# A fused attention, Fourier-mixing and gated-MLP kernel: DFT constants loaded in six pieces, the first weights' conversions and a value maximum at other steps, and the gated MLP's product on VectorE with its first tap and its cast on ScalarE

## The chip, the core and the metric

The kernel runs on one core of a Trainium2 chip. The metric is the device time of one launch in microseconds (us); lower is better. The core has a matrix engine (TensorE; PE in the profile, with PEld for its weight loads), VectorE (DVE), ScalarE (ACT), GpSimd (POOL) and a queue that only issues DMAs (SyncE, SP). Each engine takes its instructions in program order, and waits on semaphores for the others. SBUF is the on-chip memory, PSUM the memory that matmuls write.

## The reference, cut to what matters

Attention over 2 batches and 8 heads with 768 positions of width 64, where a query sees only the keys that have its own nearest centroid; then a mixing layer (two Fourier transforms, real part) with a normalised MLP; then a gated MLP.

```python
def _attn_ref(q, k, v, centroids):
    q_assign = np.argmax(np.einsum('bhsd,hcd->bhsc', q_n, c_n), axis=-1)
    k_assign = np.argmax(np.einsum('bhsd,hcd->bhsc', k_n, c_n), axis=-1)
    mask = q_assign[:, :, :, None] == k_assign[:, :, None, :]
    scores = np.where(mask, scale * np.matmul(q, k.transpose(0, 1, 3, 2)), -1000000000.0)
    attn = np.exp(scores - np.max(scores, axis=-1, keepdims=True))
    attn = attn / (np.sum(attn, axis=-1, keepdims=True) + 1e-09)
    return np.matmul(attn, v)

def _moe_ref(x, w_ch1, w_ch2):
    mixed = np.real(np.fft.fft(np.fft.fft(x, axis=1), axis=2))
    u = x + mixed
    un = (u - mu) / np.sqrt(var + 1e-06)
    return u + np.maximum(un @ w_ch1, 0.0) @ w_ch2

def _moe2_ref(x, w_in, conv_w, w_out):          # kernel = 3 taps over the sequence
    h = np.maximum(x @ w_in, 0.0)
    for k in range(K):
        conv_out += conv_w[k][None, None, :] * hp[:, k:k + S, :]
    gate = 1.0 / (1.0 + np.exp(-conv_out))
    return h * gate @ w_out
```

## The kernel before, in words

Every float32 product is made of three passes (`pass3`): each operand is split into a high part (rounded to the matrix engine's reduced float32) and a low part (what is left), and high x high, high x low and low x high are summed in PSUM.

**The attention loop** is written out by hand. It runs over steps n = -8 to 105. Of the 96 tiles (16 heads, 6 blocks of 128 queries) step n makes the scores of tile n + 8 (`score_max`: four matmuls, L530 and L532, into a PSUM slot `s`, and the row maximum by VectorE, L535, into `m`), the exponentials of tile n (`score_exp`: four matmuls, L564 and L566, into a slot `t`, read by ScalarE, L572), the split of the probabilities of tile n - 1 (ScalarE's cast L584, and the subtraction L592 by GpSimd or, for the tiles in `LO_ON_DVE`, by VectorE), and the product with V of tile n - 3 (18 small matmuls, L604). The slots for `s`, `t` and side work are three, used in turn, so a matmul into a slot waits until the slot's last reader is done. That reader is VectorE's maximum for an `s`.

Side work is hung on steps with `at(list, step, function)`; in a step the lists come in the order `pre`, `mid` (within `score_max`), `aft`, `post`, `fill`. The heads are prepared in pairs m, one pair every 12 steps (k = 12 m - 24): `load_raw` (q and k, 768 KB) at k, `prep_sims` (12 matmuls against the centroids, L404, then L408 and L410 on VectorE) at k + 5, `prep_hi` and `prep_lo` (the split of q and k; L461 and L463 on VectorE) at k + 8 to k + 11, `load_v` (384 KB into `vraw`) at k + 14, `v_max` (the largest value of V in each partition, L489 on VectorE) at k + 16, `v_turn` (a matmul that spreads it, L495) and `v_step` 0 to 3 (L502 to L508) at k + 18, `v_step` 4 and 5 (L510 on ScalarE, L512 on VectorE) at k + 22 and k + 25.

**The first weights** arrive as 64-bit numbers. Four half pieces q = 0 to 3 of two weight tiles are turned into float32 inside the loop: `ahead_start` loads a piece, five operations of `from64` (L283, L284 on VectorE, L285 on ScalarE, L286, L288 on VectorE) stand at the five steps of `AHEAD_STEPS`, and `ahead_store` writes the piece to DRAM one step later. The pieces stand in the tile `ahead`, which takes the place of `early`, the first pairs' raw and split q and k.

**The mixing** of batch 0 is hung on steps 54 to 76 (`plan`). Its constants `DC` (two planes, high and low, of 3342 columns) are loaded by GpSimd's DMA queue in the loop, and `OD` after them.

**The MLPs** follow with an automatic order. In the gated MLP, `mlp2_up(b, f)` makes one of 16 blocks of 128 hidden units: two halves of 12 matmuls each into PSUM (`u`), a relu by ScalarE into `h` (L820), three taps along the sequence into `cv` (L822 to L824), a sigmoid (L825), the product with `h` (L826), and the split into `gH` (L828) and `gL` (L829), which `down` reads in 18 matmuls (`acc`). The weights of a block are split by ScalarE (L792) and GpSimd (L794, `wlb`). `mlp2_up` runs two blocks ahead of `down`. During the first blocks `gate_in(1)` turns batch 1 (`xT`, `x`, L858 to L868), and `down` of a batch's last block copies its six results out (`y`).

## Time and profile before

| | us |
|---|---|
| median of 3 runs | 743.91 (739.0 to 745.26) |
| the profiled execution | 743.33 |
| its span, first to last instruction | 741.5 |
| PE busy in the span | 694.9 (94%) |
| DVE busy | 531.4 (72%) |
| ACT busy | 346.8 (47%) |
| POOL busy | 269.6 (36%) |
| mean granted TensorE clock | 0.984 of full speed |

The profiled execution's time is its span and 1.8 us around it. Busy time is a union of modelled intervals: matmuls overlap, so a stretch with PE busy throughout is not PE at its peak. The attention loop ends at about 296 us, batch 0 of the first MLP with the mixing of batch 1 beside it at about 395, the gated MLP starts at about 589.

### The profile page before, as it was taken

The numbers are of one execution on the slowest core, as the hardware profiler recorded it, in microseconds if no ns is written. First come the engines' busy times: TensorE is split into PE (matmuls) and PEld (weight loads), VectorE is DVE, ScalarE is ACT, GpSimd is POOL, SyncE is SP. The second block draws the span as 40 slices with busy tenths as digits, with TensorE's granted clock in tenths as the row PEclk, the third lists the DMA queues.
The fourth block names the chain that finished last, engine by engine and source line by source line (L and its number), as shares of the span: only waits on it lengthen the run. The fifth ranks groups of instructions, "written<-read, shape, count | busy, mean of one in ns | idle before, by whom it ended". The sixth has DMA issues, their size and how long they took to land.

```text
span 741.5 us, 12519 instructions
## 1 busy us (share of the span) xinstructions
PE 694.9 (94%) x5090; PEld 618.4 (83%) x5090; DVE 531.4 (72%) x753; ACT 346.8 (47%) x493; POOL 269.6 (36%) x189
## 2 busy tenths in 40 slices
PE   8898999898898998989999999999999999999996
PEld 5697788787797886878988999999999888898984
DVE  7778989799977997999389938764111268777664
ACT  3476868586457687424234423443222233333321
POOL 8064544446244454121132012222332254444441
PEclk9999999999799999999999999999999999999999
DMA  7738678463532332324013421430000000002002
GB/s 213 183 71 213 183 198 248 121 179 79 151 78 58 89 107 95 114 77 179 29 44 127 156 72 61 166 114 1 1 0 1 1 0 1 1 1 85 1 1 85
DMA packets 19937, 66.47 MB, mean 90 GB/s; under 512 B 2868, under 2 KB 5928, under 8 KB 16808
## 3 DMA queue, kind: packets, MB, share of 16 engines
q1 hardware_dynamic: 19448, 61.93, 28.9%
q0 software_dynamic: 432, 3.75, 1.5%
q8 instruction: 40, 0.66, 0.4%
q14 instruction: 17, 0.14, 0.1%
HBM read 40.94 MB, written 5.77 MB: 63 GB/s over the span
## 4 chain that ended last, share of the span: by engine, by line
PE 45%; DVE 35%; DMA 5%; POOL 5%; ACT 4%; issue 3%; SPq 1%; POOLq 0%; DVEq 0%
DVE m L535 5%; PE acc L82 5%; DVE gH L828 5%; PE acc L80 5%; PE acc L81 5%; PE up L82 5%; PE up L80 5%; PE up L81 5%; DMA vraw<-v 4%; POOL cv L826 3%; PE av L604 3%; DVE cv L823 2%; DVE cv L824 2%; PE t L564 2%; PE s L530 2%
## 5 line engine op out<-in xcount | busy, mean ns | idle before, releaser
L592 POOL TENSOR_TENSOR p<-p,p 128x768 f16<-128x768 f32 x61 | 108.3, 1778 | 113.2 <-ACT p L584 83.0
L572 ACT ACTIVATE p<-t,cbias 128x768 f32<-128x768 f32 x92 | 82.7, 899 | 51.7 <-PE t L566 50.9
L535 DVE TENSOR_REDUCE m<-s 128x1 f32<-128x768 f32 x96 | 90.1, 943 | 11.7 <-PE s L532 6.6
L80 PE MATMUL up<-un,wha 128*128 128x384 f32 x248 | 84.2, 340 | 1.5 <-DVE firste L809 0.7
L82 PE MATMUL up<-un,wla 128*128 128x384 f32 x248 | 83.9, 339 | 1.6 <-DVE wla L794 1.6
L794 POOL TENSOR_TENSOR wla<-wa,wha 128x1024 fp32r<-128x1024 f32 x16 | 38.5, 2407 | 126.5 <-ACT wha L792 126.5
L81 PE MATMUL up<-un,wha 128*128 128x384 f32 x248 | 83.8, 338 | 0.0
L809 DVE SCALAR_TENSOR_TENSOR hL<-up,hH 128x384 fp32r<-128x384 f32 x62 | 34.2, 551 | 65.5 <-ACT hH L808 65.4
L604 PEld LDWEIGHTS <-p 128*128 128x128 f16 x1728 | 60.1, 99 | 18.0 <-issue 15.5
L584 ACT CAST p<-p 128x768 f16<-128x768 f32 x88 | 73.0, 830 | 1.4
L604 PE MATMUL av<-V,p 128*128 128x65 f16 x1728 | 71.7, 196 | 2.0 <-POOL p L592 2.0
L80 PE MATMUL acc<-wha,hH 128*128 128x512 f32 x186 | 73.6, 396 | 0.0
L82 PE MATMUL acc<-wha,hL 128*128 128x512 f32 x186 | 72.6, 391 | 0.0
L81 PE MATMUL acc<-wla,hH 128*128 128x512 f32 x186 | 72.5, 390 | 0.0
L564 PE MATMUL t<-X 128*128 128x384 f32 x192 | 55.6, 371 | 15.5 <-DVE m L535 14.1
L808 ACT ACTIVATE hH<-up 128x384 fp32r<-128x384 f32 x62 | 30.5, 491 | 75.7 <-PE up L82 75.6
L530 PE MATMUL s<-X 128*128 128x384 f32 x192 | 56.8, 377 | 5.9 <-DVE m L535 4.9
L828 DVE CAST gH<-cv 128x768 fp32r<-128x768 f32 x16 | 35.4, 2212 | 31.3 <-POOL cv L826 31.3
L792 ACT CAST wha<-wa 128x1024 fp32r<-128x1024 f32 x31 | 32.6, 1050 | 52.2 <-PE acc L82 46.2
L826 POOL TENSOR_TENSOR cv<-cv,h 128x768 f32<-128x768 f32 x16 | 25.5, 1591 | 78.0 <-ACT cv L825 78.0
L564 PEld LDWEIGHTS t<-X 128*128 128x128 f32 x192 | 31.8, 193 | 24.2 <-DVE m L535 15.2
L566 PE MATMUL t<-Y 98*128 98x384 f32 x192 | 50.9, 347 | 0.1
(314 smaller groups left out, 1644.3 us busy)
## 6 DMA issues: line engine op xcount, KB each, us to landing
rawa<-w SPq DMA_DIRECT2D x14, 1024.0 KB
rawb<-w SPq DMA_DIRECT2D x8, 1024.0 KB
raw<-qk SPq DMA_DIRECT2D x7, 768.0 KB
X<-G SPq DMA_DIRECT2D x14, 384.0 KB
Y<-G SPq DMA_DIRECT2D x14, 384.0 KB
DC<-dft POOLq DMA_DIRECT2D x2, 1671.0 KB, 7.0
vraw<-v SPq DMA_DIRECT2D x8, 384.0 KB
out<-y SPq DMA_DIRECT2D x12, 256.0 KB
```

Of the source, the lines that this page charges most:

```text
L80: T.matmul(o, sH, mH, start=start, stop=False)
L81: T.matmul(o, sH, mL, start=False, stop=False)
L82: T.matmul(o, sL, mH, start=False, stop=stop)
L530: T.matmul(t[:, c, 0:384], X[:, 0, sl], X[:, 1, 384 * c:384 * c + 384], start=True, stop=False)
L535: V.tensor_reduce(m6s[h][:, i:i + 1], t[:, :, 0:384], AX.XY, ALU.max, negate=True)
L564: T.matmul(t[:, c, 0:384], X[:, 1, sl], X[:, 0, 384 * c:384 * c + 384], start=True, stop=False)
L566: T.matmul(t[:, c, 0:384], Y[0:98, 1, sl], Y[0:98, 0, 384 * c:384 * c + 384], start=False, stop=True)
L572: A.activation(p, t[:, :, 0:384], AF.Exp, bias=cbias, scale=0.125)
L584: A.copy(p16[:, 0], p32s[n])
L592: eng.tensor_sub(p16[:, 1], p, p16[:, 0])
L604: T.matmul(o, p16[:, k, 128 * j:128 * j + 128], v16[:, i, h % 2, 65 * part:65 * part + 65], start=(i + j + k + part == 0), stop=(i == 5), ...
L828: V.tensor_copy(g[0], t)
```

## The change

Four edits. The DFT constants: each plane is loaded in three pieces, at steps 8, 20, 21 and 32, 33, 44 in place of two whole planes at 20 and 32, and `OD` at 45 in place of 33. The conversions: piece 0 at steps 10, 10, 11, 11, 13; pieces 1 to 3 twelve steps earlier than before, at 17, 29 and 41 where pieces 0 to 2 stood; the loads and stores follow them. `v_max` at k + 17, `v_turn` and `v_step` 0 to 3 at k + 19, one step later each. The gated MLP: the first tap goes from VectorE's `tensor_scalar` to ScalarE's copy with a scale, the product with `h` from GpSimd to VectorE, and the cast to `gH` from VectorE to ScalarE.

```diff
-DFT_LOADS = (20, 32)
+DFT_LOADS = (8, 20, 21, 32, 33, 44)
...
-AHEAD_STEPS = [12 * q + n for q in range(4) for n in (17, 17, 18, 18, 22)]
+AHEAD_STEPS = [10, 10, 11, 11, 13] + [12 * q + n for q in range(1, 4) for n in (5, 5, 6, 6, 10)]
...
-            at(fill, k + 16, v_max, m)
-            at(mid, k + 18, v_turn, m)
+            at(fill, k + 17, v_max, m)
+            at(mid, k + 19, v_turn, m)
             for i in range(4):
-                at(aft, k + 18, v_step, m, i)
+                at(aft, k + 19, v_step, m, i)
...
             if n in DFT_LOADS:
-                i = DFT_LOADS.index(n)
-                G.dma_start(out=DC[:, i], in_=dft[:, i])
-            if n == DFT_LOADS[1] + 1:
+                i, part = divmod(DFT_LOADS.index(n), 3)
+                part = slice(*((C_CS, C_SS), (C_SS, C_CD), (C_CD, C_END))[part])
+                G.dma_start(out=DC[:, i, part], in_=dft[:, i, part])
+            if n == DFT_LOADS[-1] + 1:
                 G.dma_start(out=OD, in_=odd)
...
         t = gp.tile([128, S], F32, tag="cv", bufs=2, name=f"cv{b}{f}")
-        V.tensor_scalar(t, h2[:, 0:S], cw[:, 3 * f:3 * f + 1], None, ALU.mult)
+        A.activation(t, h2[:, 0:S], AF.Copy, scale=cw[:, 3 * f:3 * f + 1])
         V.scalar_tensor_tensor(t, h2[:, 1:S + 1], cw[:, 3 * f + 1:3 * f + 2], t, ALU.mult, ALU.add)
         V.scalar_tensor_tensor(t, h2[:, 2:S + 2], cw[:, 3 * f + 2:3 * f + 3], t, ALU.mult, ALU.add)
         A.activation(t, t, AF.Sigmoid)
-        G.tensor_mul(t, t, h2[:, 1:S + 1])
+        V.tensor_mul(t, t, h2[:, 1:S + 1])
         g = hs[1, b, f] = [gp.tile([128, S], F32R, tag=n, bufs=2, name=f"{n}{b}{f}") for n in ("gH", "gL")]
-        V.tensor_copy(g[0], t)
+        A.copy(g[0], t)
         V.tensor_sub(g[1], t, f32(g[0]))
```

Three places show what the order of instructions becomes.

VectorE at steps 52 to 54 (m is a row maximum, vsc the maximum of V, ahead the piece under conversion, mx and eq the centroid step). Before:

```order
L535 TENSOR_REDUCE m_10_2425<-s_2426 128x1
L489 TENSOR_REDUCE vsc_2466<-vraw_2385 128x1
L617 SCALAR_TENSOR_TENSOR U<-av_2163,vsc_1468,d_2387 128x6x64
L535 TENSOR_REDUCE m_10_2425<-s_2469 128x1
L283 TENSOR_SCALAR ahead<-ahead 128x512
L284 SCALAR_TENSOR_TENSOR ahead<-ahead 128x512
L408 TENSOR_REDUCE mx_2518<-sim_2505 128x24
L410 TENSOR_TENSOR eq_2520<-sim_2505,mx_2518 128x384
L535 TENSOR_REDUCE m_10_2425<-s_2527 128x1
L502 TENSOR_REDUCE vsc_2466<-s_2527 128x1
```

After the change:

```order
L535 TENSOR_REDUCE m_10_2435<-s_2436 128x1
L617 SCALAR_TENSOR_TENSOR U<-av_2173,vsc_1531,d_2397 128x6x64
L535 TENSOR_REDUCE m_10_2435<-s_2477 128x1
L408 TENSOR_REDUCE mx_2524<-sim_2511 128x24
L410 TENSOR_TENSOR eq_2526<-sim_2511,mx_2524 128x384
L489 TENSOR_REDUCE vsc_2528<-vraw_2395 128x1
L535 TENSOR_REDUCE m_10_2435<-s_2535 128x1
L535 TENSOR_REDUCE m_10_2435<-s_2574 128x1
L502 TENSOR_REDUCE vsc_2528<-s_2574 128x1
```

The maximum of V has moved behind one more row maximum and the two centroid operations, and the conversion is gone from here; in the three rounds before this one the conversion stays, and its L286 comes behind the row maximum that follows L489.

VectorE at steps 10 to 13 after the change (before, the same rows stood without the four of ahead):

```order
L535 TENSOR_REDUCE m_3_691<-s_692 128x1
L283 TENSOR_SCALAR ahead<-ahead 128x512
L284 SCALAR_TENSOR_TENSOR ahead<-ahead 128x512
L617 SCALAR_TENSOR_TENSOR U<-av_413,vsc_175,d_651 128x6x64
L535 TENSOR_REDUCE m_3_691<-s_737 128x1
L286 SCALAR_TENSOR_TENSOR ahead<-ahead 128x512
L461 TENSOR_TENSOR G_649<-raw_337,G_649 128x768
L535 TENSOR_REDUCE m_3_691<-s_790 128x1
L592 TENSOR_TENSOR p_11_796<-p_759,p_11_796 128x768
L535 TENSOR_REDUCE m_3_691<-s_824 128x1
L288 SCALAR_TENSOR_TENSOR ahead<-ahead 128x512
L512 SCALAR_TENSOR_TENSOR V_1_157<-vraw_395,vsc_525,V_1_157 128x12x64
```

Four operations are added between the row maxima of these steps.

VectorE in the last two blocks of the gated MLP, from the end of block 14 to that of block 15. Before:

```order
L828 CAST gH_7664<-cv_7658 128x768
L829 TENSOR_TENSOR gL_7665<-cv_7658,gH_7664 128x768
L822 TENSOR_SCALAR cv_7721<-h_7690,cw 128x768
L823 SCALAR_TENSOR_TENSOR cv_7721<-h_7690,cw,cv_7721 128x768
L824 SCALAR_TENSOR_TENSOR cv_7721<-h_7690,cw,cv_7721 128x768
L828 CAST gH_7727<-cv_7721 128x768
L829 TENSOR_TENSOR gL_7728<-cv_7721,gH_7727 128x768
```

After the change, on VectorE:

```order
L827 TENSOR_TENSOR cv_7662<-cv_7662,h_7631 128x768
L830 TENSOR_TENSOR gL_7669<-cv_7662,gH_7668 128x768
L824 SCALAR_TENSOR_TENSOR cv_7725<-h_7694,cw,cv_7725 128x768
L825 SCALAR_TENSOR_TENSOR cv_7725<-h_7694,cw,cv_7725 128x768
L827 TENSOR_TENSOR cv_7725<-cv_7725,h_7694 128x768
L830 TENSOR_TENSOR gL_7732<-cv_7725,gH_7731 128x768
```

and on ScalarE, from the sigmoid of block 14:

```order
L826 ACTIVATE cv_7662<-cv_7662 128x768
L829 CAST gH_7668<-cv_7662 128x768
L821 ACTIVATE h_7694<-u_7697 128x384
L821 ACTIVATE h_7694<-u_7711 128x384
L823 ACTIVATE cv_7725<-h_7694,cw 128x768
L826 ACTIVATE cv_7725<-cv_7725 128x768
L829 CAST gH_7731<-cv_7725 128x768
```

The chain of a block now changes between these two engines alone, and GpSimd has only the weights' low parts left in this stage. (Behind the constants' load, a line of the changed kernel has a number one higher: L826 to L829 of before are L827 to L830.)

## Rows read from the trace of the kernel before

**Rows 1.** The page's part 4, the chain that ended last: shares of the span by engine.

```profile
PE 45%; DVE 35%; DMA 5%; POOL 5%; ACT 4%; issue 3%; SPq 1%; POOLq 0%; DVEq 0%
```

**Rows 2.** The timeline of the matrix engine in the gated MLP: start us, duration us, the first matmul of block 15's `mlp2_up`, and the first matmul of block 14's `down`.

```profile
717.25 0.34 PE L80 MATMUL u<-x,whb 128*128 128x384 f32 x1
...
725.69 0.39 PE L80 MATMUL acc<-whb,gH 128*128 128x512 f32 x1
```

**Rows 3.** VectorE's waits for the load of V: the group in the view of waits (us in total, times, longest us), and the longest in the timeline (start us, us; in brackets the idle time before it and what ended it), at step 40.

```profile
DVE vsc L489 <- DMA vraw<-v: 13.0, 4, 4.8
```

```profile
135.57 0.95 DVE L489 TENSOR_REDUCE vsc<-vraw 128x1 f32<-128x768 f32 x1 [4.83 <-DMA vraw<-v]
```

**Rows 4.** The timeline of the matrix engine behind those waits: at step 28 (104.73), 40 (132.45, the centroid matmuls, and 137.96) and 54 to 55 (177.06).

```profile
104.73 0.62 PE L530 MATMUL s<-X 128*128 128x384 f32 x2 [0.89 <-DVE m L535]
...
132.45 2.92 PE L404 MATMUL sim<-W,raw 128*128 128x128 f32 x24
...
137.96 1.01 PE L530 MATMUL s<-X 128*128 128x384 f32 x2 [2.59 <-DVE m L535]
...
177.06 0.62 PE L564 MATMUL t<-X 128*128 128x384 f32 x2 [1.09 <-DVE m L535]
```

**Rows 5.** Busy time by stretch around step 41 and around step 58: start and end us, length, busy us (instructions) of PE, PEld, DVE, ACT, POOL, then the granted TensorE clock as a share of full speed, the DMA share and GB/s.

```profile
137.00:140.00 3.00, 2.04 (x7) 2.04 (x8) 2.93 (x6) 0.00 (x0) 0.00 (x0) 0.66 0.81 159
140.00:143.00 3.00, 3.00 (x30) 2.69 (x29) 2.45 (x8) 1.58 (x3) 0.91 (x1) 0.77 0.00 0
...
186.00:192.00 6.00, 4.07 (x26) 3.29 (x26) 5.92 (x9) 2.65 (x4) 1.65 (x1) 0.50 0.10 35
192.00:198.00 6.00, 5.97 (x38) 5.66 (x39) 4.72 (x5) 1.67 (x3) 1.88 (x2) 0.67 0.95 222
```

**Rows 6.** The timeline at steps 57 to 59: two of VectorE's operations between two row maxima, and the matrix engine behind them.

```profile
180.65 1.64 DVE L108 TENSOR_TENSOR ev<-U 128x3 f32<-128x3 f32 x1
...
183.15 2.40 DVE L463 TENSOR_TENSOR G<-raw,G 128x768 fp32r<-128x768 f32 x1
...
186.82 0.98 PE L564 MATMUL t<-X 128*128 128x384 f32 x2 [2.99 <-DVE m L535]
...
192.03 1.01 PE L564 MATMUL t<-X 128*128 128x384 f32 x2 [1.14 <-DVE m L535]
```

**Rows 7.** Busy time by stretch of the instructions of the tile `ahead` alone: DVE, ACT, then granted clock, DMA share and GB/s. The first stretch holds piece 0, the second piece 3.

```profile
70.00:90.00 20.00, 2.47 (x4) 0.64 (x1) 1.00 0.70 191
165.00:195.00 30.00, 3.90 (x4) 0.65 (x1) 0.85 0.39 100
```

**Rows 8.** The timeline at steps 11 and 12: a row maximum on VectorE with the wait before it, and the matrix engine's wait one step on.

```profile
55.60 0.96 DVE L535 TENSOR_REDUCE m<-s 128x1 f32<-128x768 f32 x1 [1.95 <-ACT ohT L431]
```

```profile
59.80 0.62 PE L564 MATMUL t<-X 128*128 128x384 f32 x2 [0.86 <-DVE m L535]
```

**Rows 9.** The page's part 6 on the constants (KB each, median us from issue to landing), and the first readers of `DC` (duration ns min/median/max, first and last start us).

```profile
DC<-dft POOLq DMA_DIRECT2D x2, 1671.0 KB, 7.0
...
OD<-odd POOLq DMA_DIRECT2D x1, 322.0 KB, 3.8
```

```profile
L80 PEld LDWEIGHTS y<-DC,EH x18: 187/188/334, 194.5 to 334.1; 128*128 128x128 f32 x18
```

**Rows 10.** The operations of a block of the gated MLP, and the two that stand nearest to the new ones on ScalarE: duration ns min/median/max, first and last start; for L454 busy us and mean ns. Then two casts in the timeline, of blocks 13 and 14.

```profile
L822 DVE TENSOR_SCALAR cv<-h,cw x16: 609/613/1690, 595.9 to 725.7; 128x768 f32<-128x768 f32 x16
L823 DVE SCALAR_TENSOR_TENSOR cv<-h,cw,cv x16: 1004/1018/3066, 596.7 to 726.4; 128x768 f32<-128x768 f32 x16
...
L825 ACT ACTIVATE cv<-cv x16: 844/846/848, 600.8 to 728.5; 128x768 f32<-128x768 f32 x16
L826 POOL TENSOR_TENSOR cv<-cv,h x16: 1544/1547/2257, 601.8 to 729.5; 128x768 f32<-128x768 f32 x16
...
L829 DVE TENSOR_TENSOR gL<-cv,gH x16: 945/958/960, 605.1 to 731.7; 128x768 fp32r<-128x768 f32 x16
```

```profile
L510 ACT ACTIVATE V<-vraw,vsc x8: 915/918/938, 14.7 to 267.2; 128x768 f16<-128x768 f32 x8
```

```profile
L454 ACT CAST G<-raw 128x768 fp32r<-128x768 f32 x7 | 5.8, 826 | 0.0
```

```profile
715.09 2.78 DVE L828 CAST gH<-cv 128x768 fp32r<-128x768 f32 x1 [2.60 <-POOL cv L826]
...
724.17 0.56 DVE L828 CAST gH<-cv 128x768 fp32r<-128x768 f32 x1 [2.60 <-POOL cv L826]
```

**Rows 11.** The matrix engine's waits in the gated MLP, from the timeline.

```profile
606.08 0.50 PE L82 MATMUL acc<-whb,gL 128*128 128x512 f32 x1 [1.06 <-DVE gL L829]
...
613.21 0.45 PE L80 MATMUL u<-x,whb 128*128 128x384 f32 x1 [0.59 <-DVE h L816]
...
641.11 0.41 PE L80 MATMUL u<-x,whb 128*128 128x384 f32 x1 [1.04 <-DVE x L868]
...
682.69 0.50 PE L80 MATMUL acc<-whb,gH 128*128 128x512 f32 x1 [1.11 <-DVE y L847]
...
731.64 0.50 PE L80 MATMUL acc<-whb,gH 128*128 128x512 f32 x1 [1.59 <-DVE gH L828]
```

**Rows 12.** The queue of DMAs that SyncE issues, around steps 6 to 10: the last move out of `early`, and the next entry.

```profile
42.14 1.10 SPq L479 DMA_DIRECT2D Y<-early  x1
...
51.97 1.60 SPq L543 DMA_DIRECT2D Y<-mr  x2
```

## The prediction

> **What bounds the kernel now.** I read the chain of waits first. It lies 45% on the matrix engine and 35% on VectorE, with DMA, GpSimd and ScalarE at 4 to 5% each [rows 1]: a kernel in which the matrix engine works nearly all the time and stops where VectorE is late. So an edit is worth what it takes out of the matrix engine's waits, and nothing more. I then listed those waits from the timeline, stage by stage, with the granted clock beside them. In the attention loop VectorE stands idle for 13.0 us until V has landed, four times, at most 4.8 us [rows 3]; what the matrix engine loses of that comes a little later and is smaller [rows 4]. In two places the clock behind a wait falls from 2.4 to 1.2 GHz, seen as a mean of 0.50 to 0.77 over some us [rows 5]: a wait can cost more than its own length. In the gated MLP a round of the matrix engine (one `mlp2_up`, one `down`) takes 8.44 us without transposes, from 717.25 to 725.69 [rows 2], and there are five waits of 0.6 to 1.6 us [rows 11].
>
> VectorE's round there is the longer one. Its five operations in order, with the wait for GpSimd's product and a cast as at 715.09, take 0.61 + 1.02 + 1.02 + 2.60 + 2.78 + 0.96 = 9.0 us [rows 10]. The matrix engine has two blocks of lead; VectorE eats it at 0.5 us a round, and the last wait, 1.59 us before the last `down`, is where the lead has gone.
>
> **The change part by part.** The sum is made against the profiled execution's 743.3 us, which lies 0.6 us under the median; I make no correction for that.
>
> *The gated MLP.* Removed: VectorE's first tap (0.61) and its cast (0.56 alone, 2.78 when it stands behind GpSimd's work on the next weights), and GpSimd's product (1.55) [rows 10]. Added on VectorE: a product of two float32 tiles, as `gL` is, 0.96. Added on ScalarE: a copy with a scale per partition, nearest L510 with 0.92, and a cast, nearest L454 with 0.83 [rows 10]; together 1.75 us of an 8.44 us round on an engine whose other work per block (two relus, a sigmoid, the weights' cast) is under half of it. The length of a block's chain hardly changes: 0.61 + 1.02 + 1.02 + 0.85 + 1.55 + 0.56 + 0.96 = 6.6 before, 0.92 + 1.02 + 1.02 + 0.85 + 0.96 + 0.83 + 0.96 = 6.6 after. What changes is VectorE's round: 1.02 + 1.02, then the sigmoid's 0.85, 0.96, the cast's 0.83, 0.96, so 5.6 us and some hand-overs, under the matrix engine's 8.44. The next block's taps no longer stand behind a cast that waits for GpSimd, and the lead stays. The five waits of [rows 11] each end on a VectorE result that is late for this reason (`gL`, a freed buffer behind it, `x`, `y`, `gH`): 1.06 + 0.59 + 1.04 + 1.11 + 1.59 = 5.4 us go. The rest of the stage is the matrix engine's own work and stays. Bounds: 3.2 if the waits on `x` and `y` remain, 6 if smaller ones go too. ScalarE's cast waits for VectorE's product with the next block's relus queued behind it; the relus have some 4 us before their PSUM bank is wanted again (half a round), so I cost that at nothing; without that cover each us of it would come 16 times.
>
> *The maximum of V, one step later.* The load has one step more, and behind `eq` the maximum also waits for the centroid matmuls, which end well after the data have come: at step 40 at 132.45 + 2.92 = 135.4 against a landing at 135.57 [rows 3, 4]. So VectorE's wait of 13.0 us nearly goes, but the row maximum behind it now also stands behind those matmuls. I walked through step 40 to 42: matmuls to 135.4, mx and eq to 136.5, the maximum of V to 137.4, the next row maximum to 138.3, wanted at about 138.1. So the matrix engine's wait of 2.59 becomes 0.1 to 0.3, and the clock does not fall: behind that wait it was 0.66 and 0.77 over 3 us each, (0.34 + 0.23) x 3 = 1.7 us [rows 5]. That place gives 2.6 + 1.7 - 0.1 = 4.2 (bounds 1.5 and 4.3). The wait at step 28 gives 0.9 [rows 4]. At steps 5 and 65 nothing waited for V, and there the later place only puts one 0.95 us reduction [rows 3] between the centroid step and a row maximum: up to 0.95 each, I take 0.5, so 1.0 lost.
>
> *The conversions.* Piece 3 leaves steps 53 to 58, where VectorE was busy 3.90 us with it; a piece alone takes 2.47 [rows 7]. VectorE has no slack there: 5.92 of 6 us are busy from 186 to 192 [rows 5]. The wait of 1.09 at 177.06 stands right behind its L286, and goes [rows 4]. Of the 1.14 at 192.03 [rows 6] I take off one operation of about 0.7, so 1.8 us in all (bounds 0.7 and 2.2). The wait of 2.99 at 186.82 I leave. It comes of two operations of step 57, a fold of 1.64 + 0.95 and a low part of 2.40 [rows 6], between the same two row maxima, and the change touches neither. Piece 0 comes to steps 10 to 13, where the matrix engine already waits 0.86 for VectorE [rows 8]. VectorE gets 2.47 to 3.90 us more there [rows 7], and 1.95 us of idle time, until ScalarE has released a bank, covers the first half [rows 8]. I take 1.0 us lost (bounds 0 and 2.6: all covered, or 3.90 less what that idle time covers and a little more).
>
> The SP queue: `ahead_start` of piece 0 must wait until the last move out of `early`, issued at 42.14, has landed. Nothing stands behind it until 51.97 [rows 12], so it delays nothing. Its store is put ahead of the load of V at step 14, 256 KB more before that load, which the extra step of the maximum covers; without it V would be about 1 us later there.
>
> *The constants.* Six DMAs in place of two. A plane of 1671 KB lands in 7.0 us and `OD`'s 322 KB in 3.8 [rows 9]; on that line a piece of about 557 KB takes 3.8 + 235 x 3.2 / 1349 = 4.4 us. All are issued by step 45, and the first reader starts at 194.5 [rows 9], at step 60. I cost it at nothing, -0.5 to +0.5: no matrix engine wait in the list ends on these DMAs, and GpSimd has idle time for four more issues.
>
> The sum: gated MLP -5.4; V -4.2 - 0.9 + 1.0; conversions -1.8 + 1.0; constants 0. That is -10.3, and **743.3 - 10.3 = 733.0 us**.
>
> **The rivals.** *The burst at step 57 goes too.* If VectorE meets GpSimd's operations at another moment there, its fold and low part take 0.95 us each as such operations do alone [rows 10], the wait of 2.99 ends, and the half clock behind it, (0.50 + 0.33) x 6 = 5.0 us [rows 5]: 733.0 - 8.0 = 725. For it: 1.64 us for a 128x3 operation is a wait, not work. Against it: the steps, the order and GpSimd's load there are the same.
>
> *The loop gives nothing.* The centroid matmuls and the split of q and k set the loop's pace as VectorE's next lateness, and waits of the same size come back within the same 12 steps. Then only the gated MLP counts: 743.3 - 5.4 = 737.9. For it: the matrix engine's waits are far smaller than VectorE's 13 us. Against it: 2.59 us at step 40 has no other reason than V.
>
> *The product on VectorE meets GpSimd's weight split.* Where they overlap now, the cast takes 2.78 in place of 0.56 [rows 10], so 2.2 us more; a tap took 3.07 in place of 1.02 [rows 10], so an operation with two inputs pays too. A round with that is 5.6 + 2.2 = 7.8 us, with `x` 8.5: as long as the matrix engine's, and the waits on `x` and `y` stay, 733.0 + 2.2 = 735.2. Against it: ScalarE casts the weights after the sigmoid, for about 1 us, and the 0.96 us product starts at once. The Trainium skill (SBUF — State Buffer, "SBUF: two separate sides") speaks for this rival: VectorE's operations with two SBUF inputs and GpSimd's share a pair of ports under an exclusive lock, and the loser blocks for the whole instruction, so moving the cast to ScalarE frees VectorE while the product brings it back under the lock. The 2.78 against 0.56 agrees.
>
> *Slower.* At steps 17 to 19 of each of four rounds, L489 and L286 now stand before the row maxima that follow the centroid step. If GpSimd holds L286 off as it did with piece 3 (1.4 us more [rows 7]), the matrix engine waits 2 to 3 us, and the clock falls behind it as at steps 41 and 58. A place then costs 2.6 + 1.7 = 4.3 to 3.0 + 5.0 = 8.0 [rows 4 to 6], four places 17 to 32, in place of the loop's gain of 4.9: 743.3 - 5.4 + 17 to 32 = 755 to 770. It decides where a wait reaches the 2.6 to 3.0 us behind which the clock fell.
>
> **How the numbers follow.** Forecast 733, chance 0.52, itself 728 to 737 by its bounds; burst gone 725, 0.17; loop gives nothing 738, 0.19; product blocked 735, 0.08; slower 755 or more, 0.04. A measurement of this kernel tells about 1% (7.4 us) from no change, so the line is 736.5. Faster by more: 0.48 + 0.17 + 0.06 + 0.03 = 0.74; within: 0.22; slower: 0.04. The range 724 to 740 leaves out half of the burst's case, the slower one and a little of the third.
>
> **What would show it.** Right: no wait for V over 1 us on VectorE; no lowered clock around step 41; `gL` of the last block ready before block 14's `down` ends, and no matrix engine wait over 0.7 us after 605. Wrong: a matrix engine wait of 2 us at steps 10 to 13 or 17 to 20 with a clock below 1; VectorE's product at 2 us or more in most blocks; relus in the gated MLP that end later than half a round after their matmuls.

## The result, and the profile after

The changed kernel takes 731.59 us (median of 4 runs, 729.77 to 731.75) against 743.42 for the kernel before beside it (739.0 to 745.26): a ratio of 0.985, 95% interval 0.981 to 0.988, 11.8 us less where the prediction had 10.3. The profiled execution after took 731.62 us, its span 729.9.

| | before | after |
|---|---|---|
| PE busy, us (share of the span) | 694.9 (94%) | 690.8 (95%) |
| DVE busy | 531.4 (72%) | 526.4 (72%) |
| ACT busy | 346.8 (47%) | 376.1 (52%) |
| POOL busy | 269.6 (36%) | 245.9 (34%) |
| mean granted clock | 0.984 | 0.992 |

The chain of the page after, by engine, answers to [rows 1]:

```profile
PE 64%; DVE 26%; issue 3%; DMA 2%; POOL 2%; ACT 2%; SPq 1%; DVEq 0%; POOLq 0%; ACTq 0%
```

The matrix engine has 64% of the chain in place of 45%, VectorE 26% in place of 35%. To see where the time went I cut each trace at markers that every kernel has: the centroid matmuls (L404) of steps 5, 17, 29, 41, 53 and 65, the first matmul of the gated MLP, and the last matmul. After, the timeline of the matrix engine has the markers of steps 53 and 65 here (start us, duration us):

```profile
165.54 2.70 PE L404 MATMUL sim<-W,raw 128*128 128x128 f32 x22
...
208.24 2.03 PE L404 MATMUL sim<-W,raw 128*128 128x128 f32 x16
```

The segments, in us, worked out from such rows; "same loop" is the mean of the five traces of kernels whose loop is that of before (before and the runs e1, e5, e6, e7 below), with their lowest and highest. Of its first row, e1, e6 and e7 have 0.8 us in a wait for a DMA of `Y` near step 15, which before and e5 do not have:

| segment | before | same loop | after | after less before |
|---|---|---|---|---|
| steps 5 to 17 | 30.66 | 31.05 (30.66 to 31.31) | 32.84 | +2.2 |
| 17 to 29 | 30.94 | 31.21 (30.82 to 31.87) | 30.40 | -0.5 |
| 29 to 41 | 31.53 | 31.90 (31.53 to 32.26) | 31.06 | -0.5 |
| 41 to 53 | 34.69 | 32.90 (31.35 to 34.69) | 31.09 | -3.6 |
| 53 to 65 | 45.34 | 45.37 (43.70 to 46.24) | 42.70 | -2.6 |
| 65 to the gated MLP | 376.53 | | 376.83 | +0.3 |
| gated MLP | 147.30 | | 139.61 | -7.7 |

Up to step 5 the trace after is 0.8 us longer; the last section shows where that comes from.

**The gated MLP after.** Of the waits in [rows 11] none is left. The only wait with a name in the stage is one that was there before, for the first block's weights; the matmuls of [rows 2] stand here 9.2 us earlier, still 8.44 us apart:

```profile
587.56 0.44 PE L82 MATMUL u<-x,wlb 128*128 128x384 f32 x1 [1.63 <-POOL wlb L795]
...
708.08 0.34 PE L80 MATMUL u<-x,whb 128*128 128x384 f32 x1
...
716.52 0.39 PE L80 MATMUL acc<-whb,gH 128*128 128x512 f32 x1
```

The groups of instructions of that stretch after (busy us, mean ns, then the idle time before them and what ended it):

```profile
L830 DVE TENSOR_TENSOR gL<-cv,gH 128x768 fp32r<-128x768 f32 x16 | 32.2, 2015 | 11.8 <-ACT gH L829 11.8
...
L827 DVE TENSOR_TENSOR cv<-cv,h 128x768 f32<-128x768 f32 x16 | 15.3, 958 | 9.6 <-ACT cv L826 9.6
```

The product takes 0.96 us on VectorE in each of the 16 blocks and is never held up; on ScalarE the copy with a scale takes 0.94 and the cast 0.83, as costed. `gL`, 0.96 us before [rows 10], now takes 2.0 in the mean. What stood beside GpSimd's weight split has moved by one operation, and no matmul waits for it.

**The loop after.** Around step 41 the clock is 1.00 where [rows 5] has 0.66 and 0.77; around step 58 it still falls (windows: from:to, length, busy us of PE, PEld, DVE, ACT, POOL, then the clock):

```profile
137.00:140.00 3.00, 3.00 (x34) 2.72 (x32) 2.97 (x5) 1.11 (x2) 1.31 (x2) 1.00 1.01 206
140.00:143.00 3.00, 2.62 (x30) 2.19 (x29) 2.90 (x8) 2.01 (x4) 2.04 (x3) 1.00 0.39 82
186.00:192.00 6.00, 3.98 (x28) 3.65 (x29) 6.00 (x7) 2.47 (x3) 1.88 (x2) 0.72 0.45 96
```

The matrix engine's waits after at steps 11 to 13, where piece 0 has come, and behind step 57 (in brackets the wait and what ended it):

```profile
58.44 0.62 PE L564 MATMUL t<-X 128*128 128x384 f32 x2 [0.94 <-DVE m L535]
61.86 0.62 PE L564 MATMUL t<-X 128*128 128x384 f32 x2 [1.10 <-DVE m L535]
64.97 0.62 PE L564 MATMUL t<-X 128*128 128x384 f32 x2 [0.77 <-DVE m L535]
...
183.26 0.59 PE L564 MATMUL t<-X 128*128 128x384 f32 x2 [2.84 <-DVE m L535]
188.02 0.62 PE L564 MATMUL t<-X 128*128 128x384 f32 x2 [2.46 <-DVE m L535]
```

At steps 11 to 13 they are 2.8 us in all; before they were 1.4, with 0.86 of it in [rows 8]. Behind step 57 they are 2.84 and 2.46, against 2.99 and 1.14 in [rows 6].

### The profile page after: what moved, and what is told of

It reads as the page before. It is cut to its first block, busy times and chain, and to the rows that moved or that the text cites. A ratio compares the mean times of both kernels' runs of the same rounds, so it can differ in the third digit from the quotient of the medians.

```text
span 729.9 us, 12502 instructions
## 1 busy us (share of the span) xinstructions
PE 690.8 (95%) x5090; PEld 618.1 (85%) x5090; DVE 526.4 (72%) x737; ACT 376.1 (52%) x525; POOL 245.9 (34%) x177
## 4 chain that ended last, share of the span: by engine, by line
PE 64%; DVE 26%; issue 3%; DMA 2%; POOL 2%; ACT 2%; SPq 1%; DVEq 0%; POOLq 0%; ACTq 0%
PE acc L80 8%; PE acc L81 8%; PE acc L82 8%; DVE m L535 6%; PE up L82 5%; PE up L80 5%; PE up L81 5%; PE av L604 3%; PE u L82 3%; PE u L80 3%; PE u L81 3%; DMA ahead<-w 2%; PE t L564 2%; PE s L530 2%; PE sim L404 2%
## 5 line engine op out<-in xcount | busy, mean ns | idle before, releaser
L795 POOL TENSOR_TENSOR wlb<-wb,whb 128x1024 fp32r<-128x1024 f32 x16 | 38.9, 2440 | 96.5 <-ACT whb L793 79.5
L532 PE MATMUL s<-Y 96*128 96x384 f32 x192 | 50.3, 343 | 0.0
```

What stands on the lines that cost most here:

```text
L532: T.matmul(t[:, c, 0:384], Y[0:96, 0, sl], Y[0:96, 1, 384 * c:384 * c + 384], start=False, stop=True)
L795: eng.tensor_sub(wl, w32[k, f], f32(wh))
```

## The experiments

The theory is the prediction's: VectorE's round in the gated MLP, V's late landing at step 40, VectorE's load at steps 10 to 13 and 53 to 58. Times are medians; ratios are to the kernel before in the same comparison.

### One edit, or one half, at a time

**e1_gate**: before, with the three lines of the gated MLP.

```diff
-        V.tensor_scalar(t, h2[:, 0:S], cw[:, 3 * f:3 * f + 1], None, ALU.mult)
+        A.activation(t, h2[:, 0:S], AF.Copy, scale=cw[:, 3 * f:3 * f + 1])
...
-        G.tensor_mul(t, t, h2[:, 1:S + 1])
+        V.tensor_mul(t, t, h2[:, 1:S + 1])
...
-        V.tensor_copy(g[0], t)
+        A.copy(g[0], t)
```

> The kernel before with the gated MLP's three edits alone. Theory (VectorE's round is shortened under the matrix engine's, the lead of two blocks stays): every matrix engine wait behind the first block's weights goes, and with each the slow first matmul behind it; the two traces side by side put that at 7.7 us from the first matmul of the gated MLP to the end, so 743.4 - 7.7 = 735.7 us, and the stage is as long as in the changed kernel, to 0.3 us. By the prediction's term alone, 5.4 us, it would be 738.0. Rival (part of the stage's gain comes from the stages ahead, that leave the engines at another distance): the stage gains 5.4 us or less here, and the loop edits alone give more than the loop.

Measured: 737.21 us, ratio 0.991 (0.988 to 0.995). In its trace the gated MLP takes 139.66 us, as in the changed kernel (139.61): 7.6 us, all of it made in the stage itself. The medians give 5.6; their interval, 4 to 9 us, holds both.

**e2_loop**: the changed kernel with those three lines as before.

> The changed kernel with the gated MLP as before: constants in six pieces, conversions and the maximum of V at the new steps. Theory: the loop's gain of 3.9 us at the gated MLP's first matmul comes back, the stage behind it is as before; 743.4 - 3.9 = 739.5 us. Rival (the loop gives nothing, what it showed is the difference between two executions): 743.4, within 1 us, and the offset at the end of the attention loop below 1.5 us. With the run of the gate alone the two gains add up to that of the whole change, 11.7 us, to 1.5 us.

Measured: 739.34 us, ratio 0.996 (0.993 to 0.998). Its segments are those of the changed kernel to 0.1 us up to step 53 (32.84, 30.34, 30.96, 30.99; then 43.26), and the gated MLP is back at 147.36. The loop gives 3.5 us by the times; with e1's 5.6 that is 9.1 of 11.8. That is 2.7 us short, more than the 1.5 expected; the intervals of the three, about 2 to 2.6 us to either side, cover it.

**e3_vmax**: before, with the maximum of V one step later.

```diff
-            at(fill, k + 16, v_max, m)
-            at(mid, k + 18, v_turn, m)
+            at(fill, k + 17, v_max, m)
+            at(mid, k + 19, v_turn, m)
             for i in range(4):
-                at(aft, k + 18, v_step, m, i)
+                at(aft, k + 19, v_step, m, i)
```

> The kernel before with the maximum of V, its spread and its steps one step later, and nothing else. Theory (V's landing holds VectorE, VectorE holds the matrix engine at step 40, and the clock falls behind that wait): the wait of 2.59 us at 137.96 goes, the granted clock from 137 to 143 is 1.00 in place of 0.66 and 0.77, VectorE's idle time on V falls from 13.0 us to under 1.5; the offset from step 29 to 53 is -3 to -5 us and the time about 743.4 - 3.5 = 740 us. Rival (the step 40 wait comes from the conversion's L286 and the centroid step on the same steps, V only happens to be named): the wait at step 40 stays over 1.5 us and the clock below 0.9 there.

Measured: 741.31 us, ratio 0.998 (0.995 to 1.000). The wait at step 40 is gone and the segment 41 to 53 is 31.00, as the theory has it; but the time moved by 1.5 us only, with an interval that reaches no change. The reason stands in the traces of the other kernels, whose loop is that of before. VectorE's load of V and the matrix engine's wait behind it at step 40, first in e1_gate:

```profile
135.28 0.95 DVE L489 TENSOR_REDUCE vsc<-vraw 128x1 f32<-128x768 f32 x1 [3.94 <-DMA vraw<-v]
...
137.67 0.61 PE L530 MATMUL s<-X 128*128 128x384 f32 x2 [1.72 <-DVE m L535]
```

and in e7_tap:

```profile
134.10 0.95 DVE L489 TENSOR_REDUCE vsc<-vraw 128x1 f32<-128x768 f32 x1 [2.95 <-DMA vraw<-v]
...
136.50 0.61 PE L530 MATMUL s<-X 128*128 128x384 f32 x2 [0.71 <-DVE m L535]
```

Five traces of that loop have 2.59, 1.83, 1.72, 1.25 and 0.71 us, with V's landing as late as VectorE's wait says. The profiled execution of before was the worst of them. Against their mean, 32.90, the later maximum is worth 1.9 us there, not 3.7. The segment 5 to 17 is 1.1 us longer than their mean, but not all of that is the maximum. The two waits of e3 there that before does not have are:

```profile
45.19 0.62 PE L564 MATMUL t<-X 128*128 128x384 f32 x2 [0.46 <-DVE m L535]
...
67.10 0.59 PE L532 MATMUL s<-Y 96*128 96x384 f32 x2 [1.13 <-DMA Y<-G]
```

The first is the row maximum that the moved reduction delays; the changed kernel has it too (0.46 at 46.53), and e8 below, with the old step for this pair, does not. The second ends on a DMA and is 0.8 us in three of the five traces with the old maximum.

**e4_conv**: before, with the conversions at the new steps.

```diff
-AHEAD_STEPS = [12 * q + n for q in range(4) for n in (17, 17, 18, 18, 22)]
+AHEAD_STEPS = [10, 10, 11, 11, 13] + [12 * q + n for q in range(1, 4) for n in (5, 5, 6, 6, 10)]
```

> The kernel before with the conversions at the new steps, and nothing else. Theory: piece 0 at steps 10 to 13 costs 1.0 us by the prediction and 1.7 to 2.2 by the trace of the changed kernel (waits for a row maximum at steps 11 to 13 grow from 1.4 to 2.8 us); piece 3 out of steps 53 to 58 gives 1.8 to 2.6; the wait for V at step 40 stays, with its lowered clock. Net 0 to -1: 742.5 to 743.5. Rival (piece 0 costs nothing, the 2.2 us lost between steps 5 and 17 come from the later maximum of V or from the constants' first piece, issued at step 8): the matrix engine's waits at steps 10 to 13 stay at 1.6 us in total and the segment from step 5 to 17 is within 0.5 us of before.

Measured: 736.06 us, ratio 0.991 (0.987 to 0.994): 6.8 us, where 0 to 1 was expected, and more than the whole loop of e2 gives. The segment 5 to 17 lost 1.6 as expected. The gain lies in 53 to 65: 38.47 us against 45.34 before and 42.70 after the whole change. The waits behind step 57 in e4:

```profile
185.10 0.58 PE L564 MATMUL t<-X 128*128 128x384 f32 x2 [1.12 <-DVE m L535]
188.80 0.62 PE L564 MATMUL t<-X 128*128 128x384 f32 x2 [1.41 <-DVE m L535]
```

What VectorE and GpSimd do there, in e4, and then in the changed kernel:

```profile
182.01 0.94 DVE L110 TENSOR_TENSOR ev<-U 128x765 f32<-128x765 f32 x1
182.86 2.46 POOL L592 TENSOR_TENSOR p<-p,p 128x768 f16<-128x768 f32 x1 [0.87 <-ACT p L584]
182.88 0.94 DVE L463 TENSOR_TENSOR G<-raw,G 128x768 fp32r<-128x768 f32 x1
```

```profile
178.72 0.94 DVE L110 TENSOR_TENSOR ev<-U 128x765 f32<-128x765 f32 x1
179.29 1.87 POOL L592 TENSOR_TENSOR p<-p,p 128x768 f16<-128x768 f32 x1 [0.59 <-ACT p L584]
179.59 2.40 DVE L463 TENSOR_TENSOR G<-raw,G 128x768 fp32r<-128x768 f32 x1
```

After the change GpSimd's subtraction comes while the fold L110 runs, goes ahead of L463, and L463 takes 2.40 us. In e4 it comes as L110 ends; L463 goes ahead in 0.94 and GpSimd's operation takes 2.46 in place of about 1.65. So less than a third of a microsecond lies between the two outcomes, and with it whether the row maximum is late. All fourteen traces agree: L463 takes 2.1 to 2.4 us in the ten where GpSimd's start is 0.10 us or more ahead of its own, and 0.94 in the four where it is at most 0.02 ahead. The window from 186 to 192 has a clock of 1.00 in e4, 0.72 after, 0.50 before [rows 5]; steps 53 to 65 start within 3.6 us of each other in the three.

**e10_const**: before, with the constants in six pieces.

```diff
-DFT_LOADS = (20, 32)
+DFT_LOADS = (8, 20, 21, 32, 33, 44)
...
```

> The kernel before with the constants in six pieces, and nothing else. Theory (no wait of the matrix engine ends on these transfers, before or after): 743 us within 1.5 us, and no segment of the loop more than 1 us off the kernel before behind step 5. Rival (six transfers at other steps collide with the loads of V, of the raw queries or of the masks, or free GpSimd for VectorE's operations at other moments): a new wait on a DMA, or waits of the row maxima at step 40 or 57 that differ by over 1 us, in either direction.

Measured: 743.82 us, ratio 1.002 (0.998 to 1.005). No change in the time, as predicted; the waits at steps 40 and 57 are 2.36 and 2.98 us. Two of the expectation's finer points did not hold: the segment 53 to 65 is 1.6 us shorter (43.72, where e1, with the old constants, has 43.70), and a wait of 1.21 us on the DMA of `Y` stands at 68.10. Such a wait is in e3 as well (1.13), with the old constants, so neither needs the six pieces.

### The three edits of the gated MLP, one alone each

Each is before with one of the three lines of e1.

**e5_product**, the product on VectorE:

> The kernel before with the gate's product on VectorE in place of GpSimd; tap and cast stay on VectorE. Theory of the round (a round of VectorE over 8.44 us eats the lead): 0.61 + 1.02 + 1.02 + 0.85 for the sigmoid + 0.96 + 0.56 + 0.96 = 6.0 us, or 8.2 where the cast still takes 2.78 beside GpSimd's weight split; under 8.44 either way, so the stage gains 5 to 7.7 us of the 7.7 that the three edits give. Rival (the cast has to leave VectorE, since it is what GpSimd holds up; the product alone brings one more operation to be held up): gain under 3 us, product or cast over 2 us in most blocks.

**e6_cast**, the cast on ScalarE:

> The kernel before with the gate's cast on ScalarE alone; tap on VectorE, product on GpSimd. Theory of the round: 0.61 + 1.02 + 1.02 + 0.85 + 1.55 + 0.83 + 0.96 = 6.8 us if GpSimd takes the product at once, and up to 2.4 more where it is still at the weights' low part; 7 to 9 us, so half of the 7.7 us, 3 to 6. Rival one (the cast that GpSimd held up was the whole loss): 7 us or more. Rival two (the product behind GpSimd's weight split sets the round): gain under 2 us, product starting over 1.5 us behind the sigmoid's end in most blocks.

**e7_tap**, the first tap on ScalarE:

> The kernel before with the first tap on ScalarE alone. Theory of the round: 9.0 - 0.61 = 8.4 us, as long as the matrix engine's 8.44, so the lead is no longer eaten but not won back either: the waits before the last product and after the copies of y shrink, gain 2 to 4 of the 7.7 us. Rival (operations on VectorE are not the limit, the chain from relu to gL is, and that stays at 6.6 us): gain under 1 us.

Measured: 736.27, 736.71 and 736.11 us (ratios 0.991, 0.992 and 0.991). The gated MLP is shorter by 6.5, 6.2 and 6.7 us; the three together give 7.7. So any one of them does nearly all of it. The time from one `gL` to the next shows why. VectorE's rows of blocks 4 to 6 in the kernel before (9.07 and 9.05 us apart), and then in e7_tap (8.42 and 8.37):

```profile
635.30 0.96 DVE L829 TENSOR_TENSOR gL<-cv,gH 128x768 fp32r<-128x768 f32 x1
644.37 0.96 DVE L829 TENSOR_TENSOR gL<-cv,gH 128x768 fp32r<-128x768 f32 x1
653.42 0.96 DVE L829 TENSOR_TENSOR gL<-cv,gH 128x768 fp32r<-128x768 f32 x1
```

```profile
630.57 0.96 DVE L829 TENSOR_TENSOR gL<-cv,gH 128x768 fp32r<-128x768 f32 x1
638.99 0.96 DVE L829 TENSOR_TENSOR gL<-cv,gH 128x768 fp32r<-128x768 f32 x1
647.36 0.96 DVE L829 TENSOR_TENSOR gL<-cv,gH 128x768 fp32r<-128x768 f32 x1
```

VectorE's round was 9.07 us against the matrix engine's 8.44 [rows 2]; with one edit it follows the matrix engine's pace. That confirms the round of 9.0, and makes my expectations for e6 (3 to 6 us) and e7 (2 to 4) too small: once the round is no longer than the matrix engine's, the lead is not eaten and the waits do not shrink by half, they go. It did not even need the cast freed; in e7 that still takes 2.21 us in the mean:

```profile
L828 DVE CAST gH<-cv 128x768 fp32r<-128x768 f32 x16 | 35.4, 2210 | 32.7 <-POOL cv L826 32.7
```

### Who undoes the conversions' gain, and what is left

**e8_vthree**: the changed kernel with the later maximum of V only where V lands late.

```diff
-            at(fill, k + 17, v_max, m)
-            at(mid, k + 19, v_turn, m)
+            late = m in (2, 3, 4)
+            at(fill, k + 16 + late, v_max, m)
+            at(mid, k + 18 + late, v_turn, m)
             for i in range(4):
-                at(aft, k + 19, v_step, m, i)
+                at(aft, k + 18 + late, v_step, m, i)
```

> The changed kernel with the maximum of V one step later only for the pairs m = 2, 3, 4 (steps 17, 29 and 41), and at its old step for m = 1, 5, 6 (steps 4, 52 and 64). Theory (the later maximum pays only where V lands late, at steps 28 and 40; for the pair at step 52 it pushes VectorE's work onto GpSimd's operations, so that the low part L463 of step 57 takes 2.40 us in place of 0.94): the matrix engine's waits of 2.84 and 2.46 us behind step 57 become 1.1 and 1.4 as with the conversions alone, the clock there stays 1.00, and the segment from step 53 to 65 is 4 us shorter than in the changed kernel, the one from step 5 to 17 0.6 us shorter; 731.6 - 4.6 = 727 us. Rival (the collision at step 57 is a matter of a fraction of a us and falls either way whatever the steps): the waits stay at 2.5 us and the time within 1 us of 731.6.

Measured: 727.01 us, ratio 0.979 (0.973 to 0.984), 4.6 us below the changed kernel. The segment 53 to 65 is 38.46, 4.2 shorter; 5 to 17 is 32.20, 0.6 shorter. Its waits behind step 57 are e4's:

```profile
182.56 0.59 PE L564 MATMUL t<-X 128*128 128x384 f32 x2 [1.11 <-DVE m L535]
186.27 0.62 PE L564 MATMUL t<-X 128*128 128x384 f32 x2 [1.42 <-DVE m L535]
```

So the whole change holds two gains that meet: with piece 3 away, L463 goes ahead of GpSimd, and the later maximum of V for the pair prepared at step 53 puts it behind again. Pairs 1, 5 and 6 were put back together here; that pair 5 is the one rests on its place, since what pair 6 moves stands behind step 63 and what pair 1 moves at steps 4 and 5; no run moves pair 5 alone.

**e9_fold53**: the changed kernel with VectorE's fold at another step.

```diff
-        plan = (("even0", fill, 54), ("even1", aft, 57), ...
+        plan = (("even0", fill, 54), ("even1", aft, 53), ...
```

> The changed kernel with VectorE's fold of the mixing (L108 to L110) at step 53 in place of 57, ahead of the centroid operations for which VectorE waited 3.08 us there; nothing else. Theory (the waits of 2.84 and 2.46 us behind step 57 come from the fold and L463 standing between the same two row maxima, each held up beside GpSimd's subtractions): L463 stands alone, at most one of the two waits stays over 1.2 us, the clock from 180 to 192 is 1.00, and the segment from step 53 to 65 is 3 to 5 us shorter than the changed kernel's 42.7 us: 731.6 - 4 = 727.6 us. Rival (the low part L463 is held up there by GpSimd whether or not the fold stands ahead of it, and the row maximum is late by that alone): a wait of 2 us or more stays, and the gain is under 1.5 us.

Measured: 726.74 us, ratio 0.977 (0.972 to 0.983): 4.9 us below the changed kernel, the segment 53 to 65 37.72. L463 is still held up, and the rival is wrong all the same:

```profile
168.50 0.94 DVE L110 TENSOR_TENSOR ev<-U 128x765 f32<-128x765 f32 x1
...
179.02 2.12 DVE L463 TENSOR_TENSOR G<-raw,G 128x768 fp32r<-128x768 f32 x1
```

```profile
186.12 0.61 PE L564 MATMUL t<-X 128*128 128x384 f32 x2 [1.42 <-DVE m L535]
```

Alone between its two row maxima, its 2.12 us leave a wait of 0.36 at 182.41; with the fold ahead of it, after the change, the wait is 2.84. The clock stays at 1.00 from 180 to 192.

**e11_both**: e8 with the fold at step 53, and the first mirrored sum of the mixing one step earlier.

```diff
-        plan = (... ("even1", aft, 57), ...
+        plan = (... ("even1", aft, 53), ...
...
-                ... ("patch", aft, 71),
-                ("ab0M", fill, 71), ...
+                ... ("patch", aft, 70),
+                ("ab0M", fill, 70), ...
```

> The kernel with V late for m = 2, 3, 4 only (727.0 us), with two more moves in the mixing of batch 0: VectorE's fold at step 53 in place of 57, and the mirrored sum of the first output pair with its patch at step 70 in place of 71. Theory: of the waits of 1.11 and 1.42 us behind step 57 one goes, 1 to 1.5 us; the wait of 2.35 us behind step 71, where L461 (2.41) and the sum (1.58) stand between the same two row maxima with VectorE idle for 1.3 us twice just before, falls below 1 us, with the clock of 0.85 over 12 us behind it: 2 to 3 us. Together 727.0 - 3.5 = 723.5 us. Rival (VectorE is full there, what is moved comes out as a wait at the next row maximum): within 1 us of 727.0.

Measured: 725.9 us, ratio 0.976 (0.973 to 0.980): 1.1 us below e8 where 3.5 was expected, so close to the rival's "within 1 us". The wait of 2.35 us behind step 71 in e8, and what stands there in e11:

```profile
232.41 1.01 PE L564 MATMUL t<-X 128*128 128x384 f32 x2 [2.35 <-DVE m L535]
```

```profile
230.64 0.62 PE L564 MATMUL t<-X 128*128 128x384 f32 x2 [0.88 <-DVE m L535]
237.00 0.59 PE L530 MATMUL s<-X 128*128 128x384 f32 x2 [0.72 <-DVE m L213]
```

0.88 and 0.72 in place of 2.35, and from step 65 on the trace is 1.1 us shorter. At step 57 the two waits became one of 1.95, 0.5 us less. So part of the moved work did come back as a wait at a later row maximum, as the rival has it.

**e12_piece0**: e11 with piece 0 spread further.

```diff
-AHEAD_STEPS = [10, 10, 11, 11, 13] + ...
+AHEAD_STEPS = [10, 10, 11, 16, 16] + ...
```

> The kernel with V late for three pairs and the two moves in the mixing (725.9 us), with the last two VectorE operations of piece 0 (L286 and L288) at step 16 in place of 11 and 13. Theory (the loss between steps 5 and 17, 1.5 to 2.2 us in all runs with the new steps, is L286's 1.78 us between two row maxima that were already late, and the subtraction L592 behind it that takes 2.33): the matrix engine's waits of 0.91, 1.11 and 0.79 us at steps 11 to 13 fall to 1.5 us in total, no wait over 0.5 us comes at steps 16 to 18, and the segment from step 5 to 17 is 1.0 to 1.5 us shorter: 724.7 us. Rival (VectorE is busy from step 10 to 18 without a gap, so 2.4 us of work come out as a wait wherever they stand): the waits move to steps 16 to 18, and the time is within 0.5 us of 725.9.

Measured: 724.47 us, ratio 0.976 (0.972 to 0.979), the shortest of all. But the reason expected is not in the trace: the segment 5 to 17 fell from 32.23 to 30.66, all that piece 0 had cost, and 17 to 29 rose from 30.39 to 32.32. The waits have moved:

```profile
59.31 0.62 PE L564 MATMUL t<-X 128*128 128x384 f32 x2 [0.51 <-DVE m L535]
73.13 0.62 PE L530 MATMUL s<-X 128*128 128x384 f32 x2 [0.73 <-DVE m L535]
```

That is the rival's mechanism: VectorE is full from step 10 to 18. From step 5 on the two traces differ by 0.1 us; the 2.1 us by which e12's profiled execution reaches step 5 earlier are the opening's (last section). The medians are 1.4 us apart, in different comparisons, so no gain of this edit is shown.

## Why the prediction was right, and where its steps were wrong

The forecast of 733.0 is 1.4 us over the time. Its sum holds, but two of its terms are off in opposite directions, by about 2 us each, and one gain was not seen: that the total is so close is in part luck.

**The gated MLP, -5.4: right in kind, too small.** The round of 9.0 us is 9.07 in the trace, and all five waits of [rows 11] are gone. Two things were left out of the sum: two smaller waits of the kernel before (0.43 at 602.09 and 0.33 at 732.71), and that each wait costs more than its length. Comparing the traces round by round, the 1.06 us wait gave 1.41, the 0.59 gave 0.85, the 1.04 gave 1.27, the 1.11 gave 1.38: 0.23 to 0.35 us more each. The rows of before around 606 us account for most of it. In a run, matmuls of 0.39 us start 0.23 us apart, so they overlap by 0.16 us. The profile counts a wait from the end of the last matmul, and that overlap is lost besides. The first matmul behind the wait is also 0.1 us longer (0.50). 6.15 us of named waits became 7.7. The upper bound of 6 was wrong for that reason. What was held up was `gL` and not the product, so the rival of a blocked product is out: the product took 0.96 us each time, and no matmul waited for `gL`. (The 2.78 against 0.56 that speaks for that rival is a cast with one input; of the rows shown, the tap's 3.07 against 1.02 is the one of an operation with two.)

**V one step later, -4.1: too large.** The mechanism is right: no clock below 1.00 around step 41, and VectorE waits for the load of V nowhere. The step that failed is the use of one execution's wait, 2.59 us with a lowered clock, as the kernel's own. At step 40, costed at 4.2, the later maximum alone gives 1.9 us against the same loop in five executions. Up to step 65 it gives about 2.1, and by the times 1.5. The two smaller terms came out as taken: the segment with step 28 is 0.9 us shorter, and at step 5 the loss is the wait of 0.46 in e3, or the 0.6 us that e8 wins back.

**The conversions, -0.8: wrong in the part left as is.** Piece 0 cost 1.6 us alone and 2.2 with V's later maximum (taken 1.0, bounds 0 to 2.6). Three VectorE operations there are held up beside GpSimd, as at steps 53 to 58 before. Here in the trace after:

```profile
54.95 2.04 DVE L284 SCALAR_TENSOR_TENSOR ahead<-ahead 128x512 int32<-128x512 int32 x1
...
58.31 1.76 DVE L286 SCALAR_TENSOR_TENSOR ahead<-ahead 128x512 uint32<-128x512 uint32 x1
...
61.73 2.32 DVE L592 TENSOR_TENSOR p<-p,p 128x768 f16<-128x768 f32 x1
```

The larger miss is at step 57. I left that wait where it was, since "the steps, the order and GpSimd's load there are the same", and gave its going 0.17. With the conversions alone it does go (e4: the segment 53 to 65 is 6.9 us shorter, where the rival's 8.0 and the 1.8 of the sum make 9.8); in the kernel as changed it stays, since V's later maximum for that pair brings it back (e8). So the sentence was right about the changed kernel, and wrong about what it rests on: the order there is not what decides. In all traces GpSimd's lead over L463 goes with it, and 0.1 us of lead is enough.

**Constants, 0**: 0 (e10). **The rivals**: the loop gives 3.5 us, so it does not give nothing; the burst stays; the product is not blocked; the slower case did not come: at steps 17 to 20 no wait of the matrix engine reaches 0.2 us, in the two rounds after it the longest there is 0.38, and the clock is 1.00. L286 takes 0.68 us at 78.74, so GpSimd does not hold it off.

Taken together, the gain of the changed kernel is 7.7 us in the gated MLP, and 4.3 in the loop against the mean of five traces of the old one.

## What to carry to other kernels

Where one engine's round is a little longer than the round of the engine it feeds, what brings it down to that pace is worth nearly everything, and the rest little (here 0.61 us off the round gave 6.7 of 7.7 us); count rounds from one result to the next, and take the cheapest edit. A wait that ends on a transfer should be read in several executions before it is priced. Two edits that each help can undo each other where they shift the same engine's work against a neighbour's; test each alone, and the pair without the overlap, before keeping both everywhere.

## What the runs showed of the hardware

**Of VectorE and GpSimd, the one that starts first is not held up, and it shows from the first 12 us on.** All kernels here have the same instructions up to there. In e2_loop VectorE's L420 starts 0.16 us before GpSimd's low part, and it is GpSimd's that takes longer:

```profile
11.61 0.56 DVE L420 TENSOR_TENSOR oh<-desc,m 128x384 f16<-128x384 f16 x1
11.77 2.07 POOL L463 TENSOR_TENSOR early<-early 128x768 fp32r<-128x768 f32 x1
```

In e10_const GpSimd's starts first, and L420 takes 1.98:

```profile
11.75 1.80 POOL L463 TENSOR_TENSOR early<-early 128x768 fp32r<-128x768 f32 x1
11.99 1.98 DVE L420 TENSOR_TENSOR oh<-desc,m 128x384 f16<-128x384 f16 x1
```

The loop's first matmul then comes at 16.9 us in place of 14.9 to 15.7. That happens in five of the fourteen traces. The trace after is one of them and before is not, which is where the 0.8 us up to step 5 come from; e11 is one and e12 is not. All five (after, e8 to e11) have the constants in six pieces, as two of the other nine do; whether that edit makes it likelier stays open.

The Trainium skill (SBUF — State Buffer, "SBUF: two separate sides") states the rule of who waits, for a VectorE operation with two inputs in SBUF and a GpSimd operation that reads SBUF: the shared pair of ports goes to whichever starts first, for the whole instruction. These rows agree; in e4 the profile puts GpSimd's start 0.02 us ahead of L463, too close for its spans to tell.

**The clock behind a wait is not fixed by the wait.** The kernels e5_product and e7_tap have the loop of before, and the same wait of 2.96 us at step 57. The window of 3 us around its end, then that wait and the next, in e5_product:

```profile
184.00:187.00 3.00, 2.41 (x22) 2.14 (x23) 2.92 (x5) 0.69 (x1) 1.64 (x1) 0.50 0.01 1
```

```profile
184.59 0.98 PE L564 MATMUL t<-X 128*128 128x384 f32 x2 [2.96 <-DVE m L535]
...
189.83 1.01 PE L564 MATMUL t<-X 128*128 128x384 f32 x2 [1.17 <-DVE m L535]
```

and in e7_tap:

```profile
184.00:187.00 3.00, 2.29 (x26) 1.84 (x26) 2.92 (x5) 0.90 (x1) 1.65 (x1) 1.00 0.01 1
```

```profile
184.50 0.59 PE L564 MATMUL t<-X 128*128 128x384 f32 x2 [2.96 <-DVE m L535]
...
189.73 0.76 PE L564 MATMUL t<-X 128*128 128x384 f32 x2 [2.94 <-DVE m L535]
```

0.50 is the lower of the two levels, 1.2 GHz. Nor does the length of a wait settle it: behind the wait of 1.72 us at step 40 of e1_gate the clock is 0.65 over 3 us, behind the 1.83 us of e6_cast it is 1.00.

At the lower clock the matrix engine's own work takes longer and its next wait for a VectorE that is full is shorter, 1.17 in place of 2.94; in both kernels the second wait ends 5.2 us behind the first. So between two such waits a lowered clock costs nothing, since the engine that is waited for sets the pace. Behind the second wait it does cost. Over the 6 us there the clock is 0.67 in e5 and 0.72 in e7, and from the end of that wait to step 65 they take 20.5 and 20.2 us. In e1_gate, with the same loop and the same 2.96 us, it is 1.00 there, and the same way takes 18.7. Of the 5.0 us that the prediction put on the half clock at step 57, the 3.0 of the first six us were therefore no price of their own, and the 2.0 of the next six were about right (1.5 to 1.8). What sets the clock in one execution and not in the other stays open here.
